# Key and query projections of an attention kernel by one level of Strassen's recursion: seven block products instead of eight, with the block sums on VectorE

## The chip, the cores and the metric

The kernel runs on one core of one Trainium2 chip. The metric is the device time of one execution in microseconds (us). A core has a matrix engine (TensorE, "PE" in the profile), a vector engine (VectorE, "DVE"), an activation engine (ScalarE, "ACT"), a general one (GpSimd, "POOL") and a sync engine ("SP") that issues most transfers. Each engine takes its own instructions strictly in program order and waits at an instruction until the semaphores it names have been reached. Only TensorE writes matrix products, into PSUM banks of 128 partitions x 512 float32 numbers; the other engines read them from there into SBUF.

## What is computed

Attention with 32 heads of 16 over 2048 rows of width 512, gated by a feed-forward branch:

```python
B, S, D = 1, 2048, 512
H = 32; Dh = D // H
xn = _layernorm(x, axis=-1)
qkv = (xn @ wqkv).reshape(B, S, 3, H, Dh)            # wqkv: 512 x 1536
p = _softmax(einsum("bhqd,bhkd->bhqk", q, k) * Dh ** -0.5)
s = einsum("bhqk,bhkd->bhqd", p, v) @ wo
h = relu(xn @ w1 + b1) ** 2                          # w1: 512 x 1792
g = silu(h @ w2 + b2)
out = x + s * g
```

The change touches only the columns of `xn @ wqkv` that make the queries and the keys.

## The kernel before

The 2048 rows are taken in four chunks of 512 (`NC`). A first stage, some 148 us long, makes everything the attention loop reads: for each chunk it normalizes the rows (`norm`, on VectorE), transposes them on TensorE (`transpose`), and projects them to values (`start_value`, `end_value`), keys and queries (`keyquery`). The results go to DRAM (`vdram`, `kdram`, `qdram`). The main loop then takes 64 turns of eight key blocks each; its second matrix product, probabilities times values, is line 572 (`values`).

Every float32 operand of a projection is split into a rounded part and a remainder, called h and l (tags `xh`/`xl`, `wf2h`/`wf2l`, `KA0`/`KA1` and so on), and a product is taken as hh + hl + lh. The inner width of 512 is four blocks of 128, so one 128 x 512 tile of keys or queries is 12 matrix instructions (`linear`, line 112). Four column groups `g`, two kinds and four chunks make 32 such tiles, 384 instructions in all. `split` evicts a tile: ScalarE casts the product from PSUM to the h part (`cast`, line 99), VectorE subtracts it for the l part (line 105), and SP stores both.

Products rotate through three PSUM tiles of two banks each (tag `S`). A key or query tile of the kernel before takes one such tile alone and uses one bank of it; the two single-bank tiles `acc` and `lin` serve as extras. The order of all instructions on all engines is the order of the Python statements: the schedule is manual. Buffers are SBUF tags; where a tag has one buffer, the next user of it waits for the last reader of the one before. The value blocks `vblocks` go round among six buffers. The loads of normalized inputs, the norms of the next chunk and its transposes are placed by hand between the key and query tiles: `parts` is a generator that does one step of a norm at each `next`.

The part of the driver loop around the change, with the lines the profile names:

Of the kernel before, what the change touches and what calls it, by code (L numbers as in the profile page):

```python
# [24 lines left out]
FT = mybir.dt.float32  # L25
FR = mybir.dt.float32r
# [48 lines left out]
def fast_path(tc, sb, ps, env):  # L75
# [27 lines left out]
    def split(hi, lo, src, heng, leng):  # L103
        cast(heng, hi, src)
        leng.tensor_tensor(lo, src, hi.bitcast(FT), op=OP.subtract)  # L105
# [9 lines left out]
    def run(gen):  # L115
        for _ in gen:
            pass
# [6 lines left out]
    b2b = t([128, D], FT, "b2b")  # L124

    xload, xnorm, wraw, wsp, xT = {}, {}, {}, {}, {}

    def load_x(c):
        for i in range(2):
            a = xload[c, i] = t([128, 2, 512], FT, f"P{4 + 2 * (c % 2) + i}")  # L130
# [25 lines left out]
    def split_w(which, ks=range(4), parts="hl"):  # L156
        if which not in wsp:
            tiles = [[t([128, 2, 512], FR, f"P{8 + n}" if which == "v" and i else f"{w_tags[which]}{p}{i}")
                      for i in range(2)] for n, p in enumerate("hl")]
            wsp[which] = [[a[k // 2][:, k % 2] for k in range(4)] for a in tiles]  # L160
        for k in ks:
            raw, (h, l) = wraw[which][k // 2][:, k % 2], (p[k] for p in wsp[which])
            if "h" in parts:
                act.copy(h, raw)
            if "l" in parts:
                pool.tensor_tensor(l, raw, h.bitcast(FT), op=OP.subtract)
# [32 lines left out]
    def xT_tiles(c):  # L199

        if c % 2:
            xT[c] = [t([128, 4, 512], FR, f"x{p}") for p in "hl"]
        else:
            xT[c] = [t([128, 4, 512], FR, f"KA{j}") for j in range(2)]

    def transpose(c, i):
        if i == 0 and c:
            xT_tiles(c)
        h, low = xT[c]
        pt = t([128, 4, 256], FT, "S")  # L210
        for j in range(2):
            for k in range(4):
                nc.tensor.transpose(pt[:, k, 128 * j:128 * j + 128],  # L213
                                    xnorm[c, i][:, j, 128 * k:128 * k + 128], ident)
        s = slice(256 * i, 256 * i + 256)
        if c:
            act.copy(h[:, :, s], pt)
        else:
            for j in range(2):
                act.copy(h[:, 2 * j:2 * j + 2, s], pt[:, 2 * j:2 * j + 2])  # L220
        for j in range(2):
            k = slice(2 * j, 2 * j + 2)
            dve.tensor_tensor(low[:, k, s], pt[:, k], h[:, k, s].bitcast(FT), op=OP.subtract)

    def transpose_tile(i):

        h, low = xT[0]
# [4 lines left out]
        act.copy(h[:, :, s], pt)  # L232
        dve.tensor_tensor(low[:, :, s], pt, h[:, :, s].bitcast(FT), op=OP.subtract)

    def xpart(c, p, k):
        return xT[c][p][:, k]

    def save_xT(c):
        for p in range(2):
            sp.dma_start(xdram[c][:, p], xT[c][p].bitcast(FT))  # L240

    def start_value(c, i, tag="S", **kw):
        pv = t([128, 512], FT, tag)
# [16 lines left out]
    def keyquery(c, g, which, tag="S"):  # L260
        pk = t([128, 512], FT, tag)
        run(linear(pk, lambda p, k: wsp[which][p][k][:, 128 * g:128 * g + 128],
                   lambda p, k: xpart(c, p, k)))
        n = 2 * g + (which == "q")
        ev = t([128, 2, 512], FR, ("P2", "P3", "P4", "P5", "P6", "P7", "T", "T")[n] if c == 3 else f"P{n % 4}")
        split(ev[:, 0], ev[:, 1], pk, act, dve)
        dst = kdram[g][c // 2][:, :, 512 * (c % 2):512 * (c % 2) + 512] if which == "k" else qdram[g][c]
        sp.dma_start(dst, ev.bitcast(FT))

    ka, qa = {}, {}  # L270

# [145 lines left out]
    def first(m):  # L417
        w, x, q = wf[1, m], xs[0], PAIRS[m][1]

        def evict():  # L420
            r = t([128, 2, 512], FT, "T")
            for f in range(2):
                dve.tensor_scalar(r[:, f], spare[:, f], b1t[:, 2 * m + f:2 * m + f + 1], 0.0, op0=OP.add, op1=OP.max)
            dve.tensor_tensor(r, r, r, op=OP.mult)
            hid[m] = [t([128, 2, 512], FR, f"h{p}{q}") for p in "hl"]
            split(*hid[m], r, dve, pool)

        return [Block(lambda p, k, f=f: w[p][:, k, 128 * f:128 * f + 128], lambda p, k: x[p][:, k],
                      range(4), evict) for f in range(2)]

    def second(c, g, i):
# [13 lines left out]
                for j in (2 * i, 2 * i + 1)]  # L445

    def load_x_parts(c):
        xs[0] = [t([128, 4, 512], FR, f"x{p}") for p in "hl"]
        for p in range(2):
            sp.dma_start(xs[0][p].bitcast(FT), xdram[c][:, p])  # L450


    fill = []
# [10 lines left out]
    load_w("k", sp)  # L464
    load_x(1)
    sp.dma_start(b1raw, b1.rearrange("(f p) -> f p", p=128))
    vblocks = [t([128, VW], FT, f"P{10 + i}") for i in range(6)]
# [46 lines left out]
    def chain(*gens):  # L514
        for g in gens:
            yield from g

    parts = chain(norm(1, (0, 1)), norm(1, (2, 3)))
    for c in range(NC):
        for i in range(4):  # L520
            if c or i > 2:
                end_value(c, i, start_value(c, i))
                if c or i == 3:
                    next(parts, None)
            if c == 0 and i == 2:
                split_w("q")
            if c == 1 and i == 0:
                bp = t([128, 14], FT, "acc")
                nc.tensor.transpose(bp, b1raw, ident[:14, :14])
                dve.tensor_copy(b1t, bp)  # L530
        if c == 3:
            act.activation(t([128, 1], FT, "warm"), eps, AF.Exp)
            for _ in range(2):
                load_piece()
        for g in range(4):
            if g == (2 if c else 3) and c + 1 < NC:
                for i in range(2):
                    transpose(c + 1, i)
                if c < 2:
                    save_xT(c + 1)  # L540
                if c + 2 < NC:
                    parts = chain(norm(c + 2, (0, 1)), norm(c + 2, (2, 3)))
            for which in "kq":
                if c == 3 and g == 3 and which == "q":
                    exps(0, 0, scores(0, 0))
                    exps(0, 1, scores(0, 1))
                keyquery(c, g, which, "acc" if (c, g, which) == (3, 3, "q") else "S")
                next(parts, None)
            if g == 0 and c + 2 < NC:
                load_x(c + 2)  # L550
            if g == 3 and c == 2:
                turn["KA"] = 1
                load_ka(0, 0)
                load_qa(0, 0)
            if g == 0 and c == 3:
                load_v(0)
            if g == 1 and c == 3:
                split_piece(act)

    load_ka(0, 1)  # L560


# [99 lines left out]

    def split_wo(i):
        if i == 0:
            wos[0] = [t([128, 4, 512], FR, f"x{p}") for p in "hl"]
        h, l = (w[:, 2 * i:2 * i + 2] for w in wos[0])
        split(h, l, woraw[i], dve, pool)
# [49 lines left out]

    def project(c, i):
        return [Block(lambda p, k, j=j: onorm[c, k][p][:, 128 * j:128 * j + 128],
                      lambda p, k: wos[0][p][:, k], range(3 if c == 2 else 4),  # L720
                      lambda: add_gated(c, i), () if c == 2 else (3,), (3,) if c == 3 else ())
                for j in (2 * i, 2 * i + 1)]

# [71 lines left out]


    n = turn["S"]
    places[:] = [(n - 2) % 3, (n - 1) % 3, n % 3]
# [6 lines left out]

    def rest(i, dst):

        group(dst, lambda p: onorm[2, 3][p][:, cut[i]], lambda p: wos[0][p][:, 3])

    def end_rest(i, src):  # L810

# [259 lines left out]
```

## Time and profile before

| what | value |
|---|---|
| median of 3 runs (lowest to highest) | 1226.03 us (1225.44 to 1226.51) |
| the profiled execution: its own time | 1225.83 us |
| its span, first to last recorded instruction | 1224.1 us |
| mean granted TensorE clock | 0.998 |

The profile is of one execution. For each engine it gives the busy time, and for each group of instructions (source line, operation, output and inputs, shape) the count, the busy time, the mean duration of one in ns, and, behind the last bar, how long the engine was idle just before them and what ended that. The chain of waits is followed back from the last instruction: at each step to what released it. A duration runs from an instruction's start to its visible result; on TensorE, ScalarE and VectorE the next independent instruction can start a little before that.

### The profile page before, as it was taken

Reading aid. Unit: us, or ns where it says so; the run is one execution under the profiler, and the core shown is the slowest. Engines: PE = TensorE matmul, PEld = TensorE weight load, DVE = VectorE, ACT = ScalarE, POOL = GpSimd, SP = SyncE. Lnnn points to the kernel's source line nnn. Section 1 sums busy time; section 2 is a strip of 40 time slices with the busy share of each in tenths; the row PEclk is TensorE's granted clock in tenths of the full one; section 3 lists DMA queues with packets and bytes.
Section 4 is the critical chain, followed back from the end, with each engine's and each line's share of the span. In section 5 each row is a group of like instructions: output and inputs, shape, how many; then the busy total and the mean of one; then the engine's idle time right before and its main releaser. Section 6 shows DMA issues by size and latency. Waiting matters only on the chain.

```text
span 1224.1 us, 24044 instructions
## 1 busy us (share of the span) xinstructions
PE 1213.3 (99%) x9925; PEld 716.3 (59%) x9925; DVE 815.8 (67%) x1302; ACT 1011.6 (83%) x1172; POOL 278.8 (23%) x222
## 2 busy tenths in 40 slices
PE   9999999999999999999999999999999999999997
PEld 8888755555555555555555555555555555555553
DVE  4542277676767775757686666676775758777776
ACT  4222489988889898888998888899898899899983
POOL 5000032122221230404022222131230403321222
PEclk9999999999999999999999999999999999999999
DMA  8675723232161223223423224151422233455434
GB/s 311 253 269 187 269 78 106 74 96 62 47 202 47 91 78 101 79 78 106 157 63 112 62 49 131 31 172 47 135 79 79 75 100 79 130 191 164 157 129 111
DMA packets 103543, 146.52 MB, mean 120 GB/s; under 512 B 42938, under 2 KB 57288, under 8 KB 101892
## 3 DMA queue, kind: packets, MB, share of 16 engines
q1 hardware_dynamic: 100772, 136.54, 35.5%
q0 software_dynamic: 2368, 7.87, 2.2%
q8 instruction: 79, 1.29, 0.4%
q10 hardware_dynamic: 288, 0.52, 0.1%
q14 instruction: 36, 0.29, 0.1%
HBM read 99.42 MB, written 45.47 MB: 118 GB/s over the span
## 4 chain that ended last, share of the span: by engine, by line
PE 99%; DVE 0%; ACT 0%; issue 0%; POOL 0%; POOLq 0%
PE acc L572 37%; PE spare L347 29%; PE S L299 15%; PE S L112 10%; PE acc L299 5%; PE lin L299 2%; PE lin L476 1%; PE S L213 1%; PE acc L112 0%; PE lin L112 0%; PE S L716 0%; DVE P L957 0%; DVE P L952 0%; PE spare L716 0%; PE S L230 0%
## 5 line engine op out<-in xcount | busy, mean ns | idle before, releaser
L303 ACT ACTIVATE P<-S 128x1024 f32<-128x1024 f32 x702 | 662.6, 1035 | 90.1 <-PE S L299 89.9
L572 PE MATMUL acc<-P,V 128*32 128x512 f32 x4096 | 453.5, 594 | 0.0
L322 DVE COPY P<-acc 128x512 f32<-128x512 f32 x322 | 222.7, 692 | 141.8 <-PE lin L299 71.3
L303 ACT ACTIVATE P<-P 128x1024 f32<-128x1024 f32 x322 | 314.5, 1082 | 0.0
L572 PEld LDWEIGHTS acc<-P,V 128*32 128x32 f32 x4096 | 126.1, 110 | 287.1 <-issue 265.5
L299 PE MATMUL S<-QA,KA 64*128 64x512 f32 x1404 | 289.7, 403 | 0.0
L322 DVE COPY P<-lin 128x512 f32<-128x512 f32 x322 | 220.5, 685 | 1.9 <-PE lin L299 0.6
L299 PEld LDWEIGHTS S<-QA,KA 64*128 64x128 f32 x1404 | 133.6, 184 | 109.8 <-issue 41.8
L105 POOL TENSOR_TENSOR wf1l<-wr,wf1h 128x1024 fp32r<-128x1024 f32 x28 | 68.4, 2443 | 289.1 <-ACT wf1h L99 112.1
L299 PE MATMUL acc<-QA,KA 64*128 64x512 f32 x322 | 127.3, 395 | 0.0
L299 PE MATMUL lin<-QA,KA 64*128 64x512 f32 x322 | 127.1, 395 | 0.0
L373 POOL MEMSET note<- 1x1 f32 x68 | 6.0, 88 | 397.7 <-PE spare L347 390.7
L347 PE MATMUL spare<-xl,wf1h 64*128 64x512 f32 x464 | 96.2, 391 | 0.0
L105 POOL TENSOR_TENSOR hl<-T,hh 128x1024 fp32r<-128x1024 f32 x28 | 80.0, 2859 | 52.9 <-DVE hh L101 51.1
L347 PE MATMUL spare<-xh,wf1l 64*128 64x512 f32 x480 | 91.6, 391 | 0.0
L347 PE MATMUL spare<-wf2l,hh 64*128 64x512 f32 x448 | 90.4, 390 | 0.0
L105 POOL TENSOR_TENSOR wf2l<-wr,wf2h 128x1024 fp32r<-128x1024 f32 x28 | 67.2, 2399 | 90.2 <-DVE wf2h L101 90.2
L598 DVE TENSOR_TENSOR ou<-acc,ou 128x512 f32<-128x512 f32 x31 | 21.4, 692 | 97.2 <-PE acc L572 85.4
L347 PE MATMUL spare<-wf2h,hl 64*128 64x512 f32 x448 | 83.5, 391 | 0.0
L347 PE MATMUL spare<-xh,wf1h 64*128 64x512 f32 x480 | 77.8, 392 | 0.0
L347 PE MATMUL spare<-wf2h,hh 64*128 64x512 f32 x448 | 72.0, 394 | 0.0
L299 PEld LDWEIGHTS acc<-QA,KA 64*128 64x128 f32 x322 | 59.3, 184 | 16.8 <-DVE P L322 2.3
(239 smaller groups left out, 1300.3 us busy)
## 6 DMA issues: line engine op xcount, KB each, us to landing
wr<-in_B_w_dram SPq DMA_DIRECT2D x56, 512.0 KB
KA<-kd SPq DMA_DIRECT2D x64, 256.0 KB
QA<-qd SPq DMA_DIRECT2D x128, 128.0 KB
kd<-P SPq DMA_DIRECT2D x15, 512.0 KB
qd<-P SPq DMA_DIRECT2D x15, 512.0 KB
u<-ud SPq DMA_DIRECT2D x15, 512.0 KB
V<-vd SPq DMA_DIRECT2D x8, 664.0 KB
vd<-P SPq DMA_DIRECT2D x16, 280.0 KB
```

Of the source, the lines that this page charges most:

```text
L105: leng.tensor_tensor(lo, src, hi.bitcast(FT), op=OP.subtract)
L112: mm(dst, lhs(a, k), rhs(b, k), start=n == 0, stop=n == len(todo) - 1)
L213: nc.tensor.transpose(pt[:, k, 128 * j:128 * j + 128], xnorm[c, i][:, j, 128 * k:128 * k + 128], ident)
L299: mm(dst, k[r, p, 128 * (kb % 8):128 * (kb % 8) + 128], q[r, p], start=True, stop=True)
L303: act.activation(ptile[i, p], src, AF.Exp, scale=SCALE)
L322: dve.tensor_copy(ptile[i, p][:, hp], sides[hp])
L347: ins = mm(bank, self.lhs(a, k)[r], self.rhs(b, k)[r], start=n == 0 and self.at[other] == 0, stop=n == len(self.todo[half]) - 1 and self.a ...
L373: f = pool.memset(note[:, notes[0]:notes[0] + 1], 0.0)
L476: mm(idle[:, :128], ident, ident, start=True, stop=True)
L572: mm(sides[0][32 * j:32 * j + 32], vq[qd][:, kb, 17 * j:17 * j + 32], ptile[i, j // 2][:, j % 2], start=first, stop=last)
L598: dve.tensor_tensor(ou, sides[0], part[0], op=OP.add)
```

## The change

Strassen's recursion (in Winograd's form) multiplies two 2 x 2 block matrices with seven block products and fifteen block sums or differences instead of eight products and four sums. Here the blocks are: two halves of the inner width (`j`), two column groups (`2p` and `2p + 1`), and two chunks of rows (c - 1 and c, with c = 1 or 3). For each of `kq` and each `p` in 0, 1:

- `first_products` makes two of the seven products from plain operands; their sum is the tile of column group `2p` and chunk c - 1. Two products (p = 0 and 1) share one PSUM tile of two banks, twice. `t1` keeps the first product for later.
- `sums_x` makes the four combinations of the transposed rows of the two chunks, for one half of the 512 rows at a time, and splits each into h and l: five sums on VectorE and one on GpSimd, four casts on ScalarE, two remainders on VectorE and two on GpSimd. `transpose` leaves an unsplit copy of odd chunks (`plain`) for it.
- `sums_w` makes the four combinations of the weight blocks: four sums on VectorE into the single buffer `gl`, one cast on ScalarE, one remainder on GpSimd. It runs for each of four kinds in each pair of chunks, eight times.
- `last_products` makes the other five products and the three remaining output tiles, with six sums on VectorE reading PSUM, and three splits.

A product of two blocks has an inner width of 256: six instructions. For each pair of chunks, kind and p there are 2 + 5 = 7 products of 6 instructions, 42, where there were four tiles of 12, 48. The driver now goes by pairs of chunks: first products of k, a transpose, sums, first products of q, a transpose, sums, two `sums_w`, the values of chunk c, and then the four `last_products`, with the other two `sums_w` behind the first two of them. The value blocks go round among three buffers instead of six, the transposed parts are four tiles instead of two, and the first loads for the main loop move: `load_v(0)` to the end of the stage.

```diff
     def transpose(c, i):
...
-        if c:
-            act.copy(h[:, :, s], pt)
...
+        halves = [pt[:, 2 * j:2 * j + 2] for j in range(2)]
         for j in range(2):
...
+            act.copy(h[j][:, :, s], halves[j])
+        if c % 2:
+            plain[c, i] = t([128, 4, 256], FT, "gl")
+            act.copy(plain[c, i], pt)
+        for j in range(2):
+            dve.tensor_tensor(low[j][:, :, s], halves[j], h[j][:, :, s].bitcast(FT), op=OP.subtract)
...
-        vb = vblocks[n % 6]
+        vb = vblocks[n % 3]
...
+    def product(dst, left, right):
+        todo = [(a, b, k) for a, b in ((0, 0), (0, 1), (1, 0)) for k in range(2)]
+        for n, (a, b, k) in enumerate(todo):
+            mm(dst, left[a][:, k], right[b][:, k], start=n == 0, stop=n == 5)
...
+    def sums_x(c, i):
...
+        sub(t1, f[:, :2], h[0])
+        sub(t1, t1, l[0])
+        sub(t2, f[:, 2:], t1)
+        sub(t3, f[:, 2:], f[:, :2], pool)
+        sub(t4, h[1], t2)
+        dve.tensor_tensor(t4, t4, l[1], op=OP.add)
+        for m, v in ((1, t2), (0, t1), (2, t3), (3, t4)):
+            act.copy(tforms[m][0][:, :, s], v)
+        for m, v, eng in ((1, t2, dve), (0, t1, pool), (2, t3, pool), (3, t4, dve)):
+            sub(tforms[m][1][:, :, s], v, tforms[m][0][:, :, s].bitcast(FT), eng)
+    def sums_w(which, p, tags):
...
+        raw = t([128, 4, 2, 128], FT, "gl")
+        s1, s2, s3, s4 = (raw[:, m] for m in range(4))
+        dve.tensor_tensor(s1, a21, a22, op=OP.add)
+        dve.tensor_tensor(s2, s1, a11, op=OP.subtract)
+        dve.tensor_tensor(s3, a11, a21, op=OP.subtract)
+        dve.tensor_tensor(s4, a12, s2, op=OP.subtract)
...
+        split(h, l, raw, act, pool)
...
+    def first_products(c, which, parts=()):
...
+        one, two = (t([128, 2, 512], FT, "S") for _ in range(2))
+        for p in range(2):
+            product(one[:, p], weights(which, 0, 0, p), xhalf(c, 0))
+            act.copy(t1[p], one[:, p])
+            firsthalf[which, p] = t1[p]
+        next(parts, None)
+        for p in range(2):
+            product(two[:, p], weights(which, 0, 1, p), xhalf(c, 1))
+            ev = t([128, 2, 512], FR, f"P{p}")
+            f = ev[:, 1].bitcast(FT)
+            dve.tensor_tensor(f, two[:, p], t1[p], op=OP.add)
+            split(ev[:, 0], ev[:, 1], f, act, pool)
+            store(which, 2 * p, c, ev)
+        next(parts, None)
+    def last_products(c, which, p, bank, temps, tags, middle=None):
...
+        product(one[:, 0], s[1], tforms[1])
+        add(u, one[:, 0], t1)
+        product(one[:, 1], s[0], tforms[0])
+        add(w, one[:, 1], u)
+        product(two[:, 0], s[2], tforms[2])
+        add(t1, two[:, 0], w)
+        keep(0, (1, 1), t1, cast_on)
+        add(u, two[:, 0], u)
+        if middle:
+            middle()
+        product(two[:, 1], s[3], xhalf(c, 1))
+        add(w, two[:, 1], w)
+        keep(1, (0, 1), w, cast_on)
+        product(five, weights(which, 1, 1, p), tforms[3])
+        add(u, five, u)
+        keep(2, (1, 0), u, cast_on)
...
+    for c in (1, 3):
+        load_x(c + 1) if c == 1 else None
+        for n, which in enumerate("kq"):
+            first_products(c - 1, which, parts)
+            next(parts, None)
+            transpose(c, n)
+            sums_x(c, n)
...
+        for i in range(2):
+            sums_w(*kinds[i], sets[c // 2][i])
...
+        values_of_chunk(c, range(4), parts)
+        for n, (which, p) in enumerate(kinds):
...
+            if c == 1 and n == 3:
+                for i in range(2):
+                    transpose(2, i)
+                save_xT(2)
...
+            last_products(c, which, p, ("acc", "lin")[n % 2], f"x{'hl'[n % 2]}0" if c == 1 else f"P{4 + n % 2}", tags,
+                          early if (c, n) == (3, 3) else None)
+            if n < 2:
+                sums_w(*kinds[n + 2], sets[c // 2][n + 2])
...
+        if c == 1:
+            values_of_chunk(2, range(4), parts)
+    load_v(0)
     load_ka(0, 1)
```

More of the change, by code (lines that the diff above doesn't have):

```diff
@@ L159, in split_w @@
                       for i in range(2)] for n, p in enumerate("hl")]
-            wsp[which] = [[a[k // 2][:, k % 2] for k in range(4)] for a in tiles]
+            wsp[which], wsp2[which] = [[a[k // 2][:, k % 2] for k in range(4)] for a in tiles], tiles
         for k in ks:
@@ L258, in end_value, with store @@
         sp.dma_start(vdram[n], vb)
[L260 to L266, printed above, removed]
+    def store(which, g, c, ev):
         dst = kdram[g][c // 2][:, :, 512 * (c % 2):512 * (c % 2) + 512] if which == "k" else qdram[g][c]
@@ new lines, in last_products, with keep @@
+    def last_products(c, which, p, bank, temps, tags, middle=None):
+        one, two, five = (t(s, FT, tag) for s, tag in (([128, 2, 512], "S"), ([128, 2, 512], "S"), ([128, 512], bank)))
+        s, t1 = sforms.pop((which, p)), firsthalf.pop((which, p))
+        both = t([128, 2, 512], FT, temps)
+        u, w = both[:, 0], both[:, 1]
+        def keep(i, half, f, eng):
+            ev = t([128, 2, 512], FR, tags[i])
+            split(ev[:, 0], ev[:, 1], f, eng, (pool, dve if middle else pool, dve)[i])
+            store(which, 2 * p + half[0], c - 1 + half[1], ev)
+        cast_on = dve if middle else act
+        add = lambda o, a, b: dve.tensor_tensor(o, a, b, op=OP.add)
+        product(one[:, 0], s[1], tforms[1])
[14 more added lines that the diff above has]
+        keep(2, (1, 0), u, cast_on)
@@ L516, in chain, with values_of_chunk @@
             yield from g
+    def values_of_chunk(c, tiles, parts):
+        for i in tiles:
+            end_value(c, i, start_value(c, i))
+            next(parts, None)
     parts = chain(norm(1, (0, 1)), norm(1, (2, 3)))
[L519 to L530, printed above, removed]
+    split_w("q")
@@ L531, in fast_path @@
         if c == 3:
             act.activation(t([128, 1], FT, "warm"), eps, AF.Exp)
[L533 to L536, printed above, removed]
-                for i in range(2):
[L538 to L551, printed above, removed]
+        if c == 1:
+            parts = chain(norm(2, (0, 1)), norm(2, (2, 3)))
```

98 lines of the change are left out of this document (71 added, 27 removed).

## The prediction

> **What bounds the kernel now.** I read the busy table first, then the chain of waits, then the table by stage.
>
> ```profile
> span 1224.1 us, 24044 instructions
> PE 1213.3 (99%) x9925; PEld 716.3 (59%) x9925; DVE 815.8 (67%) x1302; ACT 1011.6 (83%) x1172; POOL 278.8 (23%) x222
> ...
> PE 99%; DVE 0%; ACT 0%; issue 0%; POOL 0%; POOLq 0%
> ```
>
> TensorE is busy for 99% of the span and the chain that ends last is TensorE's own work. The kernel has no slack: what TensorE stops doing is gained, and every moment it waits is lost.
>
> The change lies in the first stage. Busy time by stretch (PE, PEld, DVE, ACT, POOL, then the granted clock), and two pieces of the chain:
>
> ```profile
> 48.00:75.00 27.00, 27.00 (x128) 22.57 (x128) 13.15 (x30) 6.54 (x11) 0.00 (x0) 1.00 0.63 228
> 75.00:102.00 27.00, 27.00 (x121) 22.32 (x121) 10.24 (x26) 5.09 (x10) 0.00 (x0) 1.00 0.50 196
> 102.00:126.00 24.00, 24.00 (x115) 20.14 (x114) 7.32 (x11) 5.93 (x9) 0.00 (x0) 1.00 0.63 231
> ...
> 69.28 32.69 PE S L112 x144
> ...
> 157.97 7.00 PE acc L572 x64
> ```
>
> There TensorE never waits, while VectorE and ScalarE are under half busy and GpSimd is idle. 144 projection instructions take 32.69 us, 0.227 each: a block product of six costs 1.36, a value tile of twelve 2.72.
>
> **The term that falls.** The tiles took 32 x 12 = 384 instructions; now there are 4 x 2 x 7 = 56 products of six, 336. Transposes stay. 48 x 0.227 = **-10.9 us**. This holds only if TensorE goes on without waiting.
>
> **The waits that come.** What one hand-over costs shows at a tile of before, in the timeline:
>
> ```profile
> 23.50 1.07 PE L112 MATMUL S<-KA,wf2l 128*128 128x512 f32 x4
> 24.61 0.59 ACT L99 CAST P<-S 128x512 fp32r<-128x512 f32 x1 [2.13 <-PE S L112]
> 25.23 0.69 DVE L105 TENSOR_TENSOR P<-S,P 128x512 fp32r<-128x512 f32 x1 [4.18 <-ACT P L99]
> ```
>
> The product lands at 24.57, ScalarE starts 0.04 later, VectorE 0.03 after ScalarE: I take 0.05. A matrix instruction lands 0.39 after its start, 0.17 after the next could have begun. Durations for the rest (group, mean ns; three are timeline rows):
>
> ```profile
> L105 DVE TENSOR_TENSOR P<-S,P 128x512 fp32r<-128x512 f32 x30 | 20.8, 692 | 57.6 <-ACT P L99 57.6
> L940 DVE TENSOR_TENSOR wf1l<-P,wf1h 128x256 fp32r<-128x256 f32 x2 | 0.8, 421 | 0.1
> L195 DVE TENSOR_SCALAR T<-P,mv,rs 128x512 f32<-128x512 f32 x16 | 8.1, 544 | 0.5
> L190 DVE SCALAR_TENSOR_TENSOR rs<-rs 128x2 f32<-128x2 f32 x7 | 1.1, 161 | 0.2
> 40.14 2.48 DVE L223 TENSOR_TENSOR xl<-S,xh 128x512 fp32r<-128x512 f32 x4 [0.57 <-ACT xh L217]
> L99 ACT CAST P<-S 128x512 fp32r<-128x512 f32 x30 | 17.6, 587 | 56.7 <-PE S L112 54.9 <-issue 1.7
> L164 ACT CAST hh<-wr 128x512 fp32r<-128x512 f32 x4 | 2.2, 621 | 0.0
> 136.89 1.05 ACT L99 CAST wf1h<-wr 128x1024 fp32r<-128x1024 f32 x1
> L166 POOL TENSOR_TENSOR hl<-wr,hh 128x512 fp32r<-128x512 f32 x4 | 5.0, 1308 | 0.0
> 138.01 2.40 POOL L105 TENSOR_TENSOR wf1l<-wr,wf1h 128x1024 fp32r<-128x1024 f32 x1 [112.08 <-ACT wf1h L99]
> 38.02 1.91 PE L213 MATMUL S<-ident,T 128*128 128x128 f32 x16
> ```
>
> Independent VectorE sums follow each other 0.60 apart ((2.48 - 0.69) / 3), dependent ones 0.74.
>
> (a) *Two products in one PSUM tile.* In the changed kernel's instruction order, the second product of a tile waits for the reader of the first, though it writes the other bank. A ScalarE copy between them costs 0.17 + 0.05 + 0.59 + 0.05 = 0.86, a VectorE sum 0.96, two sums 1.57. First products: `one` of k, 2 x 0.86; `two`, 4 x 0.96. Last products: the second half of `two` stands behind two sums, 8 x 1.57. Together 1.7 + 3.8 + 12.6 = **18.1**.
>
> (b) *The second half of `one`* in the eight `last_products` waits for a sum that stands in VectorE's queue behind what the call before left. X is the landing of that call's last product; TensorE is back at the wait at X - 0.17 + 1.36 = X + 1.19. First calls: 0.96 each. Else VectorE adds (X + 0.74), ScalarE casts (+0.67), VectorE subtracts (+0.74): X + 2.15. Fourth call, pair (2, 3): then the sum, X + 2.85, a wait of 1.6; in pair (0, 1) four transposed remainders (2.48) stand ahead while 16 transposes (1.75) cover part: 2.7. Third calls and the second one of pair (2, 3): `sums_w` stands ahead, four 256-wide sums of some 0.38, 1.5 in all: 3.15 each. The second call of pair (0, 1): a norm stands ahead too, whose square root is queued on ScalarE behind the 1.05 cast of `sums_w`, and whose scalings then wait for GpSimd's 2.40 (see the lock below): 1.1 + 2.4 + 1.0 more, 7.7. Sum: 1.9 + 4.3 + 9.5 + 7.7 = **23.4**.
>
> (c) *Transposes of chunk 1* wait for a norm behind the first products' sum: X + 0.74, four small steps 0.75; meanwhile ScalarE casts and GpSimd takes 1.31 to X + 2.75; only then the 0.54 scaling: a wait of 3.5, twice, **7.0**. In pair (2, 3) the norm is done earlier.
>
> (d) *First products of q.* The copy that frees `one` stands on ScalarE behind the four casts of `sums_x`, which wait for VectorE's chain. From the transposes' landing Y: three copies Y + 2.15, two remainders + 1.3, five dependent sums to Y + 7.1, the last cast and the copy 1.25: TensorE goes on at Y + 8.4, and was ready at Y + 1.2. 7.2, twice: **14.4**.
>
> (e) *The fourth value tile* takes the PSUM tile of the first, whose VectorE copy is queued behind `sums_x` and two `sums_w`. Y + 7.1 as above; remainders 0.6 and 0.65 with GpSimd's 1.3 between them; another 1.3 of GpSimd and the 1.5 of the first `sums_w` (Y + 12.4); its cast 1.1 and GpSimd's remainder 2.4 (Y + 16), because the second `sums_w` needs the single buffer `gl`; its sums 1.5 and the copy 0.7: Y + 18.2. Three value tiles cover to Y + 8.0. 10.2, twice: **20.4**.
>
> GpSimd and VectorE I let exclude one another in (b), (c) and (e). The rows: the squaring on VectorE beside GpSimd, and a sum of the same size elsewhere.
>
> ```profile
> 160.10 2.25 DVE L424 TENSOR_TENSOR T<-T 128x1024 f32<-128x1024 f32 x1
> 158.88 2.38 POOL L105 TENSOR_TENSOR wf1l<-wr,wf1h 128x1024 fp32r<-128x1024 f32 x1 [5.64 <-issue]
> L707 DVE TENSOR_TENSOR hh<-hh,T 128x1024 f32<-128x1024 f32 x5 | 6.1, 1226 | 0.2
> ```
>
> GpSimd ends at 161.26, VectorE 1.09 later: it did not begin until then. [...] Without the lock some 1.3 x 2 + 2.6 x 2 + 2.4 = 10 us of the waits would go.
>
> *The clock.* Granted clock at the very end, TensorE's last instruction, and the dummy products at the start:
>
> ```profile
> 1210.00:1220.00 10.00, 4.92 (x46) 3.25 (x37) 7.74 (x17) 0.74 (x2) 3.35 (x4) 0.93 0.75 181
> 1220.00:1224.10 4.10, 0.00 (x0) 0.00 (x0) 0.00 (x0) 0.00 (x0) 0.00 (x0) 0.50 0.07 25
> 1214.80 0.40 PE L716 MATMUL S<-QA,wf1l 128*128 128x512 f32 x1
> 1.39 6.42 PE L476 MATMUL lin<-ident 128*128 128x128 f32 x32 [1.39 <-POOL ident masks.py:199]
> 8.08 0.83 PE L476 MATMUL lin<-ident 128*128 128x128 f32 x6
> ```
>
> 0.93 over 10 us is 1.4 us at half, so the clock halved at 1218.6, 3.4 us after TensorE fell idle. Of the waits, five are well over that (d, e and the 7.7) and two touch it (c). At the start 32 dummy products took 6.42, where at the later pace ((0.83 - 0.27) / 5 = 0.11) they take 3.5: at most 2.9 lost for one cold start, nothing where the next wait hides it. I take 1.2 each for five, **6**; the bounds are 0 and 7 x 2.9 = 20. [...]
>
> *Moves at nothing.* V's first load goes to the end of the stage. In the kernel before, the stage's last product begins at 147.7 (147.06 and three more) and the first probability product at 157.97, so some 10 us cover it:
>
> ```profile
> 147.06 1.07 PE L112 MATMUL acc<-xh,hl 128*128 128x512 f32 x4
> ...
> V<-vd SPq DMA_DIRECT2D x8, 664.0 KB
> DMA packets 103543, 146.52 MB, mean 120 GB/s; under 512 B 42938, under 2 KB 57288, under 8 KB 101892
> ```
>
> At the mean rate 664 KB take 5.5 us; were the cover gone, that is the price. Three value buffers for six leave 3 x 2.72 = 8.2 us for a 280 KB store. What the added work costs VectorE, ScalarE and GpSimd in busy time is nothing by itself; it counts in the queues above.
>
> **The sum.** Waits 18.1 + 23.4 + 7.0 + 14.4 + 20.4 = 83.3; less 10.9; plus 6: +78.4. On the profiled execution's own 1225.83 us (span 1224.1; the median shown, 1226.03, is 0.2 above): **1304 us**. Nothing later gives it back, as the main loop is TensorE's too.
>
> **Rivals.**
>
> - *The sums stay hidden* (the other side). VectorE is busy 30.7 of those 78 us, and GpSimd is idle. If the queues never held TensorE it would be 1225.8 - 10.9 = 1215. It decides below 10.9 us of waits; (d) alone, two waits in which nothing but a chain of dependent sums is counted, is more. 2 in 100.
> - *Only the long queues count*: if the second bank of a tile were written without waiting, (a) and (b) go, 41.5, and perhaps the clock's 6: 1225.8 - 10.9 + 41.8 = 1257. For it: the banks are different; against it: the wait is in the instruction order. 4 in 100.
> - *A cold TensorE throughout*: in `last_products` it works 1.4 of each 2 to 4 us. If that counts as idle, its 40 products (54 us) run at half clock, and about half of the extra is hidden in the waits: +27, 1331. For it: nothing in this trace has such a pattern; against it: the clock fell only in full idleness. 8 in 100.
>
> The forecast has 86. **Range** 1276 to 1332: below, the lock gone (10), no loss by the clock (6) and hand-overs of 0.03 for 0.05, with some overlap I miss (12); above, the clock's bound or the cold rival. A difference under 0.2% is no change that could be told here. Faster 0.02, same 0.01, slower 0.97.
>
> **What would show it.** The changed stage should show TensorE idle about 83 us, in 28 gaps; in each pair ScalarE's first copy of a first product of q comes 7 us late; the fourth value tile of chunks 1 and 3 starts 10 us late behind a VectorE copy; GpSimd and VectorE alternate. The granted clock should fall below 1.0 between 30 and 220 us. The first probability product should start near 236 instead of 158, and the main loop keep its length. Wrong if TensorE's idle time there is under 40 us, or if turns of the main loop grow.

## The result, and the profile after

| | before | after |
|---|---|---|
| median (lowest to highest) | 1226.27 us (1225.44 to 1226.62), 4 runs | 1320.61 us (1319.22 to 1321.33), 4 runs |
| ratio, 95% interval | | 1.0769 (1.0750 to 1.0788) |
| span of the profiled execution | 1224.1 us | 1318.9 us |
| mean granted TensorE clock | 0.998 | 0.973 |
| first probability product | 157.97 us | 252.77 us |
| span behind it | 1066.1 us | 1066.1 us |

The change costs 94.3 us, and all of it lies ahead of the first probability product, which comes 94.8 us later; the main loop keeps its length. From the page of the changed kernel, and its chain of waits:

```profile
span 1318.9 us, 24224 instructions
...
PE 1229.9 (93%) x9877; PEld 719.0 (55%) x9877; DVE 881.8 (67%) x1398; ACT 1036.0 (79%) x1211; POOL 344.8 (26%) x259
...
PE 84%; DVE 2%; ACT 1%; issue 1%; POOL 1%; DMA 1%; SPq 0%; DVEq 0%; ACTq 0%; POOLq 0%
```
```profile
252.77 7.00 PE acc L699 x64
```

TensorE was busy for 99% of the span, now for 93%. It has 1318.9 - 1229.9 = 89.0 us without work where it had 10.8. Yet it is also busy 16.6 us longer than before, with 48 instructions fewer: most of the 94.8 us is idle time, the rest is work that takes longer.

One row for each kind of wait, from TensorE's timeline of the changed kernel (start, length, instructions; in brackets the idle time ahead and what ended it):

```profile
27.52 1.20 PE L273 MATMUL S<-KA,wf2h 128*128 128x512 f32 x4 [0.85 <-DVE P L340]
32.39 1.55 PE L215 MATMUL S<-ident,T 128*128 128x128 f32 x8 [3.22 <-DVE T L196]
84.23 0.72 PE L273 MATMUL S<-xh,KA 128*128 128x512 f32 x2 [1.38 <-DVE xh L359]
96.56 2.93 PE L273 MATMUL S<-y,P 128*128 128x512 f32 x6 [7.90 <-DVE xl L359]
162.04 2.08 PE L273 MATMUL S<-KA,hh 128*128 128x512 f32 x4 [7.34 <-ACT ou L333]
188.43 1.22 PE L112 MATMUL S<-wf1h,xh 128*128 128x512 f32 x2 [9.91 <-DVE P L101]
251.80 0.50 PE L406 MATMUL S<-QA,KA 64*128 64x512 f32 x2 [2.42 <-DMA KA<-kd]
```

There are 28 such gaps in the stage, at the places that the prediction names, 75.6 us in all. The last row is one that it does not name. The row at 96.56 shows the other half: six instructions in 2.93 us, 0.49 each for 0.23. The granted clock (the last figure but two of a row) by stretch:

```profile
50.00:80.00 30.00, 17.77 (x63) 14.01 (x64) 20.98 (x39) 8.25 (x13) 10.40 (x7) 0.77 0.36 144
80.00:125.00 45.00, 27.66 (x107) 20.49 (x106) 22.96 (x41) 9.81 (x16) 12.48 (x8) 0.85 0.36 136
240.00:270.00 30.00, 27.35 (x233) 16.63 (x236) 21.49 (x32) 24.85 (x28) 4.95 (x4) 1.00 0.41 129
```

It is below 1 through most of the stage, and back at 1.00 when the main loop starts. Laid on the moments at which it changes, 3.41 us apart, the same view reads:

```profile
107.91:111.33 3.42, 0.96 (x4) 0.83 (x5) 2.37 (x6) 1.05 (x1) 0.41 (x1) 1.00 0.79 277
111.33:114.74 3.41, 3.41 (x10) 2.34 (x8) 0.69 (x1) 0.00 (x0) 1.98 (x1) 0.50 0.96 333
114.74:118.15 3.41, 2.03 (x9) 1.49 (x9) 1.38 (x3) 0.62 (x1) 1.30 (x1) 1.00 0.02 7
...
203.49:206.90 3.41, 1.25 (x6) 0.68 (x4) 2.63 (x7) 0.62 (x1) 1.27 (x1) 1.00 0.51 190
206.90:210.31 3.41, 2.69 (x6) 2.15 (x7) 0.67 (x2) 1.04 (x1) 2.19 (x1) 0.50 0.93 309
210.31:213.73 3.42, 2.80 (x7) 1.65 (x5) 1.27 (x2) 0.00 (x0) 0.18 (x1) 0.50 0.76 243
213.73:217.14 3.41, 2.64 (x11) 2.17 (x12) 1.40 (x3) 0.79 (x2) 1.30 (x1) 1.00 0.31 117
217.14:220.55 3.41, 1.78 (x8) 1.13 (x6) 2.22 (x5) 1.07 (x2) 1.29 (x1) 1.00 0.51 194
```

Read the first number behind the comma (TensorE's busy time) against the clock of the next row. After 0.96 and 1.25 us of work the next stretch runs at 0.50; after 2.03 and 1.78 at 1.00. In a stretch that is itself at half clock I count work half (two projection instructions start 0.85 us apart there, 0.45 at full clock): after 2.69 (1.35 at full speed) the clock stays at 0.50, after 2.80 (1.40) it returns. In the whole stage 19 stretches are at half clock, and TensorE worked 41.6 us in them, of which I count half, 20.8 us, as lost speed.

That leaves VectorE and GpSimd. Both, from 155.9 us on, in the input sums of the second pair:

```profile
155.95 1.27 POOL L293 TENSOR_TENSOR P<-gl 128x512 f32<-128x512 f32 x1 [0.60 <-ACT gl L223]
...
157.16 0.68 DVE L293 TENSOR_TENSOR P<-gl,KA 128x512 f32<-128x512 f32 x1
...
160.55 1.33 POOL L293 TENSOR_TENSOR y<-P,y 128x512 fp32r<-128x512 f32 x1 [3.33 <-ACT y L301]
160.67 1.76 DVE L293 TENSOR_TENSOR u<-P,u 128x512 fp32r<-128x512 f32 x1
...
161.84 1.73 POOL L293 TENSOR_TENSOR P<-P,P 128x512 fp32r<-128x512 f32 x1
162.35 1.77 DVE L293 TENSOR_TENSOR V<-P,V 128x512 fp32r<-128x512 f32 x1
```

A difference that takes VectorE 0.68 alone takes 1.76 when GpSimd began 0.12 earlier: GpSimd ends at 161.88, and 0.55 later VectorE ends.

### The profile page after: what moved, and what is told of

Its sections match the earlier page's. It is cut to its first block, busy times and chain, and to the rows that moved or that the text cites. A ratio compares the mean times of both kernels' runs of the same rounds, so it can differ in the third digit from the quotient of the medians.

```text
span 1318.9 us, 24224 instructions
## 1 busy us (share of the span) xinstructions
PE 1229.9 (93%) x9877; PEld 719.0 (55%) x9877; DVE 881.8 (67%) x1398; ACT 1036.0 (79%) x1211; POOL 344.8 (26%) x259
## 4 chain that ended last, share of the span: by engine, by line
PE 84%; DVE 2%; ACT 1%; issue 1%; POOL 1%; DMA 1%; SPq 0%; DVEq 0%; ACTq 0%; POOLq 0%
PE acc L699 34%; PE spare L454 26%; PE S L406 13%; PE acc L406 4%; PE S L273 3%; PE lin L406 2%; PE S L112 1%; DVE P L359 0%; DMA KA<-kd 0%; DVE P L293 0%; POOL P L105 0%; ACT P L99 0%; SPq L383 0%; DMA kd<-P 0%; PE acc L273 0%
```

## The experiments

The expectations call the prediction's terms by its letters. Each experiment is compared with the kernel before, run on the same chip beside it (median 1225.7 to 1226.5), and through that with the changed kernel. Line numbers in an experiment's rows are its own.

**The clock: e1 and e2, e5 and e6.** Products nobody reads, in front of the instructions that wait:

```diff
+    def busy(place, c, bank="lin"):
+        n = dummies.get((place, c), 0)
+        if n:
+            d = t([128, 512], FT, bank)
+            for _ in range(n):
+                mm(d[:, :128], ident, ident, start=True, stop=True)
...
+        busy(f"{m}a", c, bank)
         product(one[:, 1], s[0], tforms[0])
```

> The changed kernel with 564 dummy products of 128 columns put into TensorE's 28 gaps (about 0.8 of each gap's length), into a PSUM bank that is free at that point; nothing else moves. Theory: the trace of the changed kernel shows 19 stretches of 3.41 us at half clock between 30 and 215 us, in which TensorE worked 41.6 us; half of that, 21 us, is lost to the clock. With the gaps filled the granted clock should stay at 1.00 from 25 us on, the gaps' ends stay where VectorE and ScalarE put them, and the time should fall by 18 to 28 us from 1320.6, to 1293 to 1303. Rival: the clock costs the 6 us of the prediction and the rest is waiting for VectorE: then 1312 to 1317. Second rival: the dummies delay the work behind them: no gain, 1320 or more.

> As e1, but dummies only in the 23 gaps under 4 us (271 of them); the five long gaps (5.7 to 9.9 us) stay idle. Theory: the clock is set for one fixed stretch of 3.41 us by how much TensorE worked in the stretch before (it fell after stretches with 1.34 us of full-speed work or less, and stayed after 1.40 or more), so short gaps that lie close together halve it too; in the changed kernel's trace 19.1 us of work lay in half-clock stretches that follow gaps under 4 us. Expect about 9.6 us less than 1320.6, 1309 to 1313, and the half-clock stretches left only around the five long gaps. Rival: the clock falls only in full idleness of over 3.4 us, as the prediction had it: then nothing is gained, 1319 to 1322.

Both missed: 1347.37 us and 1336.19 us, ratios 1.0984 and 1.0896. One row of e1's timeline says why:

```profile
37.87 9.54 PE L274 MATMUL lin<-ident 128*128 128x128 f32 x84
```

Here 42 dummies were laid out for 4.5 us. Each is two instructions, and 84 of them take 9.54: 0.227 for a dummy, twice what I took from the rows of the dummy products at the start. They were longer than the gaps, so that they delayed what they should only have covered. The two runs say nothing of the clock's price, and were made again with the right count.

> As e1, with the dummies counted by what e1 showed: a dummy of 128 columns is two instructions and takes 0.226 us, twice what e1 was laid out for, so that e1's dummies were longer than the gaps they should fill. Now 256 of them, 0.75 of each gap. Theory (21 us of the time are lost to half clock in 19 stretches of 3.41 us): granted clock 1.00 from 25 us to the end of the stage, the gaps' ends where they were, 18 to 28 us less than the changed kernel's 1320.6: 1293 to 1303. Rival (the clock costs the 6 us of the prediction, the rest is waiting for VectorE and ScalarE): 1312 to 1317.

> As e2 with the right count: dummies (126 of 0.226 us, 0.75 of each gap) only in the 23 gaps under 4 us. Theory (the clock for a fixed stretch of 3.41 us follows from the work in the stretch before it, with a bound near 1.37 us of full-speed work, so that gaps of 2.4 to 3.3 us can halve it): 9.6 us less, 1308 to 1314, half clock left only at the five long gaps. Rival (only idleness of over 3.4 us halves it, as the prediction had it): 1319 to 1322.

Measured: e5 1308.85 us (1308.32 to 1311.09; ratio 1.0683, 1.0667 to 1.0700), 11.8 less than the changed kernel; e6 1315.05 us (1313.97 to 1315.31; ratio 1.0725, 1.0708 to 1.0741), 5.6 less. Windows of e5, then of e6:

```profile
80.00:125.00 45.00, 40.57 (x239) 34.77 (x239) 23.93 (x44) 10.77 (x18) 13.81 (x9) 1.00 0.49 184
125.00:145.00 20.00, 19.60 (x95) 16.18 (x94) 10.08 (x26) 4.92 (x10) 2.62 (x3) 1.00 0.31 122
145.00:170.00 25.00, 22.74 (x128) 19.59 (x127) 15.56 (x19) 10.33 (x18) 11.12 (x9) 0.93 0.21 83
170.00:190.00 20.00, 17.31 (x106) 15.11 (x104) 8.43 (x16) 4.83 (x7) 6.14 (x3) 0.91 0.15 57
```
```profile
170.00:190.00 20.00, 10.09 (x35) 7.89 (x34) 11.75 (x19) 6.24 (x9) 8.74 (x5) 0.74 0.17 65
190.00:240.00 50.00, 47.20 (x267) 37.87 (x267) 26.25 (x45) 16.19 (x21) 16.34 (x11) 1.00 0.58 200
```

In e5 two half-clock stretches are left (25 x 0.07 x 2 = 3.5 us, and 3.6), which hold 6.8 us of work, so that 3.4 of the 20.8 us of lost speed remain and 17.4 are gone. The clock's part of the time, as far as dummies could take it away, is 12 us: twice the 6 of the prediction, and well under the 18 to 28 I expected. What is lost in speed isn't all lost in time. A dearer product shortens the wait behind it where that wait is set by VectorE's queue: idle time and dummies together last 23.6 + 61.8 = 85.4 us in e5 (the dummies from the first start to the last end, place by place), where the changed kernel idles 78.2 (the 75.6, the load's 2.4 and a 0.2). Of the 17.4 us, some 7 are taken back in this way.

In e6 the clock is 1.00 from 190 to 240 us, where the changed kernel had 0.90 and no gap over 2.9, and half clock is left only around the long gaps. So short gaps halved the clock too; the rival, that full idleness of over 3.4 us is needed, is out (it gave 1319 to 1322). Their part is 5.6 us, under the 9.6 of the expectation for the same reason.

**A PSUM tile for each product: e3.**

```diff
-        one, two = (t([128, 2, 512], FT, "S") for _ in range(2))
+        one = [t([128, 512], FT, tag) for tag in ("S", "S")]
+        two = [t([128, 512], FT, tag) for tag in ("lin", "acc")]
...
-        one, two, five = (t(s, FT, tag) for s, tag in (([128, 2, 512], "S"), ([128, 2, 512], "S"), ([128, 512], bank)))
+        one = [t([128, 512], FT, "S") for _ in range(2)]
+        two, five = [t([128, 512], FT, "S"), t([128, 512], FT, "lin")], t([128, 512], FT, "acc")
```

> The changed kernel with a PSUM tile of its own for each product (first products: two S tiles, lin and acc; last products: three S tiles, lin and acc), so that no product waits for the reader of another half of its tile. Theory: the terms (a) and (b) of the prediction (18.1 and 23.4) are mostly this; some of what stands in VectorE's queue comes back as a wait one tile later. Expect 30 to 38 us less waiting, and with the short gaps 8 to 12 us of the clock: 1271 to 1283. Rival: VectorE and ScalarE are what TensorE waits for in any case, the shared tile only says where: under 12 us gained, 1309 to 1321.

1276.20 us (1275.84 to 1276.58), ratio 1.0408 (1.0391 to 1.0426): 44.4 less than the changed kernel, as expected. TensorE's idle time in the stage falls from 78.2 to 46.0 us, and the clock's mean rises from 0.973 to 0.982. The 22 gaps of (a) and (b) are gone, and in the two functions three others are left, 2.47, 1.98 and 0.64. The two gaps of (d) are gone too: what waited there was the second product of q in the tile `one`, for the copy of the first. These 24 gaps were 50.7 us; 18.5 us of idle time are new. So most of that cost was where a product was put, not what VectorE had to do. Some of it comes back one place later:

```profile
48.16 1.94 PE L215 MATMUL S<-ident,T 128*128 128x128 f32 x8 [8.88 <-DVE T L196]
...
155.97 1.22 PE L112 MATMUL S<-wf1h,xh 128*128 128x512 f32 x2 [11.03 <-DVE P L101]
```

Those two waits were 3.31 and 9.91. TensorE comes to them earlier, and VectorE doesn't.

**The order of the weight sums: e4.**

```diff
+        sums_w(*kinds[0], sets[c // 2][0])
         for n, which in enumerate("kq"):
             first_products(c - 1, which, parts)
...
-        for i in range(2):
-            sums_w(*kinds[i], sets[c // 2][i])
...
         values_of_chunk(c, range(4), parts)
+        sums_w(*kinds[1], sets[c // 2][1])
```

> The changed kernel with the first weight sum of each pair moved ahead of that pair's first products and the second one behind the value tiles, instead of both ahead of the value tiles. Theory: term (e), 20.4 us, is the value copy of the first tile standing behind two weight sums in VectorE's queue; with them gone it stands behind the input sums alone, and the two waits at the fourth value tile fall from 8.4 and 9.9 to under 4.5 each, of which some comes back at other places. Expect 8 to 14 us less waiting and up to 5 less by the clock: 1303 to 1313. Rival: the chain of input sums alone holds the fourth value tile (the weight sums run in VectorE's idle time): 1318 to 1321.

1314.82 us, with a wide spread (1311.14 to 1318.87); ratio 1.0729 (1.0698 to 1.0759), 5.8 less: between theory and rival. The waits at the fourth value tile fell from 8.40 and 9.91 to 1.32 and 3.33, more than expected. But this row is new:

```profile
28.29 1.22 PE L273 MATMUL S<-KA,wf2h 128*128 128x512 f32 x2 [4.92 <-ACT P L333]
```

The cast of the early weight sum (1.04 us, from 26.71 on) now stands on ScalarE ahead of the copy that the first products wait for; the two waits are 4.92 and 2.04, for 0.68 each. Of 13.7 us 6.5 are left, and term (e) is confirmed as what stands in the queue, not as something to be had by moving it.

**GpSimd's part of the input sums on VectorE: e11.**

```diff
-        sub(t3, f[:, 2:], f[:, :2], pool)
+        sub(t3, f[:, 2:], f[:, :2])
-        for m, v, eng in ((1, t2, dve), (0, t1, pool), (2, t3, pool), (3, t4, dve)):
+        for m, v, eng in ((1, t2, dve), (0, t1, dve), (2, t3, dve), (3, t4, dve)):
```

> The changed kernel with the three GpSimd instructions of each sums_x (one difference, two remainders) on VectorE. Theory (a GpSimd instruction and a VectorE instruction with two SBUF operands exclude one another, so that VectorE loses GpSimd's 1.3 us for each in any case and does the same work itself in 0.69): the waits hardly move, 1317 to 1322. Rival (the two run side by side): twelve instructions of 0.69, 8.3 us, are added to the chains that the copies and the value tiles wait behind, of which half or more lands in the time: 1324 to 1329.

1319.05 us (1318.63 to 1320.49), ratio 1.0764 (1.0748 to 1.0781), as expected. Twelve more instructions on VectorE cost nothing. The group that stood behind GpSimd, in the changed kernel and then in e11:

```profile
L293 DVE TENSOR_TENSOR u<-P,u 128x512 fp32r<-128x512 f32 x4 | 7.1, 1767 | 0.0
```
```profile
L293 DVE TENSOR_TENSOR u<-P,u 128x512 fp32r<-128x512 f32 x4 | 2.7, 684 | 0.0
```

In the second pair's first input sums VectorE needs 156.10 to 162.58, 6.5 us, where it needed 157.16 to 164.12 with GpSimd's help. On these operands the two engines didn't work side by side.

**The late load of keys: e7.** `load_ka(0, 1)` ahead of `load_v(0)`.

> The changed kernel with the second load of keys issued ahead of V's first load, as it was before the change. Theory: in the changed kernel a score product at 251.8 us waits 2.42 us for that load, which is issued 9 us ahead of it behind V's load on SyncE's queue; with the order turned this wait goes and V is still there in time: 2.0 to 2.6 us less, 1318 to 1318.6. Rival: the queue is busy with the stores before it and V's load is what comes late then, or the wait is made up for by the exponentials behind it: 1320 to 1321.

1321.12 us (1318.69 to 1322.68), ratio 1.0771 (1.0756 to 1.0786): nothing gained, as the rival had it. The wait for the keys is gone, and in its place a score product waits 1.05 for the exponentials and the first probability product 1.47 for V, which comes last now. In the changed kernel SyncE issued these loads one behind the other, V's at 242.80 us and the keys' from 243.24 on, right behind the stage's last store (242.39); turning two of them changed who waits.

**A version laid out by the waits: e8, e9, e12.** Chunks 0 and 1 as before, Strassen for the pair (2, 3) alone, with e3's tiles and TensorE work put in front of each sum:

```diff
+        for g in range(4):
...
+            for which in "kq":
+                keyquery(c, g, which)
+                next(parts, None)
...
+    values_of_chunk(2, range(1), parts)
+    run(parts)
+    c = 3
+    for n, which in enumerate("kq"):
+        first_products(c - 1, which, parts)
+        transpose(c, n)
+        for i in ((1, 2), (3,))[n]:
+            end_value(2, i, start_value(2, i))
+        sums_x(c, n)
```

> A version laid out by what the waits show: chunks 0 and 1 by the tiles of the kernel before, Strassen's products for the pair (2, 3) alone; a PSUM tile for each product; both norms of chunk 3 and two of the four weight sums done while chunks 1 and 2 are multiplied; three value tiles of chunk 2 kept back to stand ahead of the input sums; the fourth value tile of chunk 3 in another bank; the key load ahead of V's. It saves 24 instructions, 24 x 0.227 = 5.4 us. Theory: the waits are a matter of what stands in VectorE's and ScalarE's queues and go when other TensorE work is put in front of them; 2 to 3.5 us of waits stay (a remainder on GpSimd, the last scores behind VectorE), the clock stays 1.00: 2 to 3.4 us less than before, 1222.8 to 1224.5. Rival: the sums of one pair alone still hold TensorE (half of the 76 us of the change, less the 36 of the shared tiles, is 20): 1232 to 1242.

1232.01 us (1231.24 to 1233.62), ratio 1.0051 (1.0038 to 1.0065). The waits of the sums are about as low as expected (3.6 us with the last scores', for 2 to 3.5). What misses is this, from its waits and its windows:

```profile
PE acc L710 <- DMA V<-vd: 2.3, 1, 2.3
PE S L416 <- DMA KA<-kd: 1.6, 1, 1.6
```
```profile
160.00:180.00 20.00, 18.25 (x142) 9.87 (x142) 10.04 (x15) 12.01 (x15) 4.20 (x3) 0.84 0.17 54
```

Two loads came late, and the idle time they made halved the clock in the main loop: 20 x 0.16 x 2 = 6.4 us at half. Next, the loads ahead of the last products, V's buffer freed for it:

```diff
-            for m, tags in enumerate((("y0", "y1"), ("u0", "u1"), ("P14", "P15"), ("V0", "V1"))):
+            for m, tags in enumerate((("y0", "y1"), ("u0", "u1"), ("P14", "P15"), ("T0", "V1"))):
...
+        if n == 0:
+            load_v(0)
...
         if n == 3:
+            load_ka(0, 1)
```

> The version e8 with V's first load issued ahead of the last products (its buffer no longer holds an operand of these) and the second key load ahead of the last of the four calls; the first value tile of chunk 3 in a bank of its own too. In e8 the waits that had been laid out for were gone, but V and the keys came 3.85 us late (1.59 and 2.26), and the half clock that followed cost some 3 us in the main loop's first 20 us. Theory: both go, and what is left is 5.4 us saved against some 3 us of short waits: 1223 to 1226. Rival: the loads, stores and weight pieces of this stretch fill the DMA queues (0.94 of them busy from 140 to 160 us in e8), so that what is loaded earlier makes something else late: 1228 to 1232.

1227.60 us (1226.41 to 1228.91, 11 runs), ratio 1.0014 (1.0005 to 1.0023), between theory and rival: the waits for loads are gone, but the rival has a part, since the stores that now go behind the keys are late:

```profile
146.41 3.07 ACT L420 ACTIVATE P<-S 128x1024 f32<-128x1024 f32 x3 [2.29 <-DMA qd<-P]
...
147.40 0.50 PE L416 MATMUL acc<-QA,KA 64*128 64x512 f32 x1 [1.28 <-DVE P L369]
...
152.06 0.69 DVE L439 COPY P<-acc 128x512 f32<-128x512 f32 x1 [2.33 <-DMA qd<-P]
...
152.81 0.49 PE L416 MATMUL acc<-QA,KA 64*128 64x512 f32 x1 [1.22 <-DVE P L439]
```

The exponentials write into buffers whose last content is still to be stored. Hence other buffers:

```diff
-        tags = ("P10", "P11", "P12") if n == 3 else [f"P{(3 * n + m) % 4}" for m in range(3)]
+        tags = ("P8", "P13", "T1") if n == 3 else ("P10", "P11", "P12") if n == 2 else [f"P{(3 * n + m) % 4}" for m in range(3)]
...
-            split(ev[:, 0], ev[:, 1], f, eng, (pool, dve if middle else pool, dve)[i])
+            split(ev[:, 0], ev[:, 1], f, eng, (pool, pool, pool if middle else dve)[i])
...
+        if not middle:
+            keep(1, (0, 1), w, cast_on)
         product(five, weights(which, 1, 1, p), tforms[3])
         add(u, five, u)
+        if middle:
+            keep(1, (0, 1), w, cast_on)
```

> The version e9, changed at its last two calls alone: their results go to buffers that the first exponentials don't need (in e9 ScalarE waited 2.29 us and VectorE 2.33 us for the stores of q that these buffers held), in the last call the sum that frees the bank acc stands ahead of the eviction before it, and the remainders of the last call are on GpSimd. Theory: of e9's 3.8 us of short waits some 0.8 stay; with 5.4 saved the first value product comes at about 154.5 us (157.97 in the kernel before, 158.3 in e9) and the time is 3 to 4 us under that of before, 1222 to 1223.2. Rival: the scores before the main loop are held by the exponentials themselves or by the loads, whatever the buffers: 1225 to 1228.

1223.67 us (1222.69 to 1224.51, 11 runs) beside 1225.91 of the kernel before: ratio 0.9982 (0.9973 to 0.9991). This version is faster than the kernel before by 1.1 to 3.3 us (the interval), under 0.3%, and a little above the 1222 to 1223.2 expected. Its waits, and its first probability product:

```profile
PE S L281 <- POOL P L105: 0.7, 1, 0.7
PE acc L419 <- DVE P L442: 0.4, 1, 0.4
```
```profile
154.22 7.00 PE acc L715 x64
```

With 1.1 us of waits left the product comes 3.75 us earlier than in the kernel before, of 5.4 saved. The medians differ by 2.2. The profiled execution took 1222.69 us, the lowest of the eleven times; what makes the others longer was not tried.

**Both pairs, laid out the same way: e10.** e3 and e4, the norm of chunk 1 ahead of the first products, value tiles of chunks 0 and 2 kept back as in e8.

> Both pairs by Strassen's products, with all that the waits suggested: a PSUM tile for each product, the weight sums apart, the norm of chunk 1 ahead of the first products, value tiles of chunks 0 and 2 kept back as cover between transposes and input sums, the key load ahead of V's. Theory: some 24 us of waits are left of the change's 76, most of them in the first pair, where the kernel's start leaves nothing to put in front of the sums; with the 10.9 saved, 3 to 4 for V's late load and 4 to 8 for the clock: 1242 to 1252, slower than before. Rival: as in e3 what is taken from one wait comes back at the next one, and no more than e3's gain is had: 1265 to 1280.

1251.62 us (1249.83 to 1254.75), ratio 1.0219 (1.0202 to 1.0236), as expected. 23.6 us of gaps are left, 14.7 of them ahead of 80 us, in the first pair; the longest is this:

```profile
30.26 2.08 PE L273 MATMUL acc<-KA,wf2h 128*128 128x512 f32 x4 [6.83 <-DVE b1t L638]
```

A small copy of b1 stands behind the norm that was moved ahead. In the first pair the norms, the weight splits and the sums all fall into the same 60 us. Strassen's saving there is 5.4 us, and these gaps alone are nearly three times that.

## Why the prediction came out

The time, 1320.61, is inside the range and 16.6 us above the value of 1304; on the profile the first probability product is 94.8 us late, against +78.4. The range reached that far because its upper end took in the bound of the clock and the rival of a cold TensorE, and the clock is where most of the difference lies. Step by step:

| term | predicted | gaps of the changed kernel, with 0.17 of landing for each |
|---|---|---|
| products | -10.9 | -10.9 |
| (a) two products in one tile, 14 gaps | 18.1 | 15.8 + 2.4 = 18.2 |
| (b) second half of `one`, 8 gaps | 23.4 | 22.0 + 1.4 = 23.3 |
| (c) transposes behind a norm | 7.0 | 6.5 + 0.3 = 6.9 |
| (d) copy behind the input sums' casts | 14.4 | 13.0 + 0.3 = 13.3 |
| (e) fourth value tile | 20.4 | 18.3 + 0.3 = 18.7 |
| clock | 6 | 12 (e5), some 20.8 of speed |
| loads behind the stage | 0 | 2.4 |

**The waits** were right in place, number and cause. All 28 are there, and the long ones end with the instruction that the prediction names: 7.90 for 7.7, 5.65 and 7.34 for 7.2, 8.40 and 9.91 for 10.2. The prediction counts from the moment at which TensorE could have gone on, the profile from the landing of its last instruction, hence the 0.17. The agreement is a little kinder than it should be: the sum was made for a TensorE at full speed, and there e5 shows some 88 us (85.4 less the load's 2.4 and a 0.2, and 28 landings of 0.17), 4 more than the 83.3.

**The clock** is the term that was mis-sized. The step that failed is "Of the waits, five are well over that (d, e and the 7.7) and two touch it", with 1.2 for each of five, the author's estimate under a bound of 2.9 a gap. It took from one row, at the end of the kernel, that the clock falls 3.4 us after TensorE goes idle. The runs show something else: in six traces the clock of a stretch of 3.41 us on a fixed grid followed from the work done in the stretch before, and less than 1.35 us of work there was followed by half clock every time. That the one row gave 3.4 us was a matter of where the grid lay: in the changed kernel the fall comes 2.9 us after the last product (1309.91 and 1312.82) and 4.4 us into the gap ahead of 162.04 (154.70 and 159.11). So gaps of 2.4 to 3.3 us counted (e6: 5.6 us), and a long gap cost up to three stretches (the clock is at half from 66.95 to 77.19). The rival of a cold TensorE had this idea, "1.4 of each 2 to 4 us", but as all or nothing, +27; e5 shows about half of that. The price of one gap couldn't be read off its length, since it hung on where the grid lay. The 32 dummy products of the rows from the start are 16 of two instructions each, as e1 shows; the 2.9 us taken from those rows don't depend on that.

**The loads.** "V's first load goes to the end of the stage" was set at nothing, with the stage's last 10 us as cover. V did come in time; the key load that stands behind it on SyncE's queue did not, and e7 shows that the place in the queue only decides which of the two is late.

**The lock** between GpSimd and VectorE held: e11, and the rows at 160.55, where VectorE's 0.68 alone became 1.76 behind GpSimd's 1.33. VectorE ended 0.55 after GpSimd there (162.43 and 161.88), so it had done little until then; what held it was not shown.

**The shared tile** ("if the second bank of a tile were written without waiting, (a) and (b) go", the rival at 1257): it was not written without waiting (the 22 gaps of (a) and (b), 37.8 us), and e3, which gives each product its own tile, shows what that is worth: 44 us with the clock. The rival's price left out (d), which stands on the same wait.

What stays open: about 2 us of the 94.8 have no place in this account (-10.9 + 80.4 + 20.8 + 2.4 = 92.7), and whether e4's spread of 7.7 us comes from the place of the grid was not tried.

## What to carry to other kernels

Where an engine is busy for 99%, an edit that takes 1% of its work away and makes it wait for others must be paid in waits below that 1%: count the hand-overs first, in the queues of the engines that answer, and give each product its own PSUM tile (44.4 us here, e3). Put independent work of the bound engine ahead of every hand-over before asking whether the saving is real; where there is such work (the second pair, e12) the same algebra gained 2 us, and with the first pair too, where there is little (e10), it lost. Idle time on TensorE was paid twice here, once as itself (75.6 us in 28 gaps) and once as the clock of what followed (12 us by e5).

## What the runs showed of the hardware

- **In these runs the granted clock changed on a fixed grid of 3.413 us.** In the changed kernel the ten falls ahead of the main loop, from 32.82 to 206.90 us, lie on it (51 stretches from the first to the last). With windows laid on such a grid e2, e3, e4, e6 and e7 too show only 1.00 and 0.50, with 32 falls more. With TensorE's busy time counted at its granted speed, in these six traces every stretch with less than 1.35 us was followed by half clock, and from 1.36 to 1.42 both occur (full after 1.36 and half after 1.39 in e7, half after 1.42 in e2); in e5 half clock followed some 1.5 us (work from 179.17 on, slow from 180.66 on). That is 40 to 44% of a stretch. Above that the clock was full, with one exception that stays open: in e8 a stretch with 1.82 us, all of it products of 64 rows, was followed by half clock (159.50 us). Gaps of 2.4 to 2.9 us were enough: in the changed kernel the falls at 111.33, 124.98 and 206.90 us follow stretches whose idle time belongs to a single gap, of 2.88, 2.41 and 2.88 us.
- **Part of the lost speed was no lost time.** Of 20.8 us of speed counted as lost e5 took away 17.4 by keeping TensorE busy, and 12 came back, since waits that other engines set shrink when TensorE is late.
- **A float32 dummy of 128 columns was two instructions and took 0.227 us at full clock** (e1, 84 instructions in 9.54), as much as one instruction of 512 columns on the split operands (0.227, 144 in 32.69).
